# Columns 2 and 3 of Q, K and V in blocks 0 and 1 as seven block products

## The chip, the cores and the metric

The program runs on one core of one Trainium2 chip. The metric is the device time of one execution in microseconds (us). It is given as the median of three runs; a separate execution was taken with the hardware profiler.

## What is computed

One layer on x of 2048 tokens and 576 columns: a layer norm without weights, then sliding attention and a feed-forward part side by side, both added to x.

```
xn = (x - mean(x)) / sqrt(var(x) + 1e-5)
qkv = xn @ wqkv                       # 576 x 1728; 32 heads of 18 columns
# each token looks at itself and at the tokens 2, 4, ... 14 before it
o = softmax(q . k[idx] * 18 ** -0.5) @ v[idx]
h = relu(xn @ w1 + b1) ** 2           # 576 x 4608
out = x + o @ wo + h @ w2 + b2        # 4608 x 576
```

All values are float32. The products run in the type fp32r with each operand split into a high part (a copy in that type, made by ACT) and a low part (the rest, a subtraction on DVE). One product of A and W is then three matmuls: high by high, low by high and high by low.

## The kernel before

**Tiles.** The tokens are four blocks b of 512, and Q, K and V four groups g of 8 heads, 432 columns each (QW). The normalized block stands transposed in X[b], with 4 parts of 128 of the contraction (c), high and low, and in x4[b] with the 64 columns that are left over, high and low behind each other. The tokens j of 128 within a block are four column tiles. One (b, g, j) is a *row*: a PSUM tile of 128 tokens by 432 columns, made by 4 x 3 matmuls on X[b] and 2 on x4[b], 14 in all (row_products, qkv_row). ACT copies it out of PSUM (qkv_out, L358) and writes it to the array kvq in DRAM on its own DMA queue (L360). Attention reads it back from there.

**Order of work.** All engines run in the order in which the code is written. The function open_rows starts: it normalizes block 0 from rows and makes (0, 0), with TensorE transposes (L1434) and products (L1472). q0 follows, and makes in its list todo the rows of (0,1), (0,3), (0,2), (1,3), (1,2), (1,1) and (1,0), one at a time; behind each it takes steps of its list pieces: the statistics of block 1, the split of the weights of a group (split_wq), the normalization (normalize), the four sums for the feed-forward part (sums), and the left-over columns of the first feed-forward weights (left_w). The last two rows stand in the function filler and are made within the first feed-forward pair.

**Mean and scale of block 1.** statistics(1) makes mean and inverse deviation of each token, 4 rows of 128 tokens, on DVE and POOL. turn_mr transposes the 8 columns on TensorE (L204), ACT copies them out (L206), a DMA writes them to DRAM (L207), and load_mb (L213) reads them back in all 128 partitions, as the tile mb. normalize(1) subtracts and multiplies with mb.

**Block products.** The feed-forward part (ffn_pair, 18 pairs p for each half s of the tokens) computes 2 x 2 blocks with 7 products and not 8, named T1, B11, T2, T3, B21, B22 and T4 for the weights' block in each. sums(s) makes the sums of the tokens that they need (SS[1] to SS[3] and fourth_sum), left_x and left_w the same for the left-over columns, which are written to DRAM as a stack of seven (L612) and read again by load_stack (L619). For blocks 2 and 3, quad_step makes Q, K and V in the same way, for two groups at a time (k, which is 0 or 1) and a pair of column tiles (half) at a time: 14 steps of a product and a column tile, each product 6 matmuls, and 2 for the left-over columns in four of them (L1103, L1107). phase_b0 runs it; its lists say after which steps a piece of attention is taken.

**Attention.** One (b, g) is a generator of 19 pieces, nearly all on DVE; side(n) takes n of them, and in each feed-forward pair p of the first half PIECES[p] of them are taken ahead of the second product, with 4 more later in the pair. offer(b, g) queues one group, fetch loads its tiles when one of the three kv tiles is free.

**Loads around it.** On SP's queue stand, among others, the load of the left-over columns of w1 for the next four pairs (load_left_w, L626, into tile st), the load of the left-over x (load_left_x) and of the stacks, the loads of w1 and w2 (L500, L536), and the writes of the split w1 (L521).

## Time and profile before

| | us |
|---|---|
| median of three runs | 1102.49 |
| lowest, highest run | 1099.86, 1103.36 |
| span of the profiled execution | 1098.5 |
| TensorE busy in it | 1092.3 |
| DVE, ACT, POOL busy in it | 879.9, 563.2, 149.3 |

The span is one execution from the first instruction to the last. PE is TensorE's matmuls, PEld its weight loads, DVE the vector engine, ACT the scalar engine, POOL GpSimd, SP the engine that issues most DMAs; SPq, ACTq and POOLq are their DMA queues. A row of the timeline has the start, the duration (of several instructions together where it ends in x and a number), the engine, the line of the kernel and the tiles, out<-in. In brackets stands the idle time ahead of it and what ended it. A row of the groups has all instructions of one line and shape: busy time, mean duration in ns, and the idle time before them with what ended it. A row of a tile has the least, mean and greatest duration in ns. A row of the DMAs has the queue, the number of issues, the size of each and the median time from issue to landing. The granted clock of TensorE was full in this execution from the first slice to the last. The regions that the change touches are these:

```profile
0.00:20.90 20.90, 18.61 (x90) 14.12 (x91) 13.97 (x39) 12.15 (x27) 11.03 (x28) 1.00 0.86 312
20.90:92.40 71.50, 71.50 (x368) 68.59 (x367) 57.16 (x80) 30.94 (x53) 3.35 (x6) 1.00 0.77 257
92.40:109.20 16.80, 16.80 (x79) 14.62 (x78) 9.72 (x15) 9.41 (x15) 0.00 (x0) 1.00 0.66 232
109.20:141.50 32.30, 32.13 (x142) 26.18 (x141) 31.36 (x43) 22.16 (x29) 12.83 (x24) 1.00 1.02 341
```

The columns are the window and its length, the busy time of PE, PEld, DVE, ACT and POOL, the granted clock, the share of the DMA engines and GB/s. The first window is the start (open_rows), the second the rows of q0 but for the last two, the third the first feed-forward pair with those two rows, the last the two pairs behind it. TensorE waits 0.17 us in the fourth window and nothing in the second and third.

### The profile page before, as it was taken

To read this page: it belongs to the slowest core of one execution; us is meant where nothing else is said; L and a number is where in the kernel's file an instruction comes from. 1 tells how busy PE (TensorE), PEld (TensorE's weight loads), DVE (VectorE), ACT (ScalarE), POOL (GpSimd) and SP (SyncE) were. 2 spreads that over 40 slices of the span, in tenths; PEclk is the share of its full clock that TensorE was granted. 3 is DMA by queue.
4 is the path that set the end of the run, shared out by engine and by line. 5 is a ranking of instruction groups with operands and counts; after the bars stand their busy time and mean duration, and the time that the engine had idled before them with its cause. 6 is when DMAs were issued, how large, how long until landed. Compare 5 with 4: busy or idle time off the path is not lost.

```text
span 1098.5 us, 13947 instructions
## 1 busy us (share of the span) xinstructions
PE 1092.3 (99%) x4936; PEld 922.9 (84%) x4936; DVE 879.9 (80%) x1183; ACT 563.2 (51%) x794; POOL 149.3 (14%) x267
## 2 busy tenths in 40 slices
PE   9999999999999999999999999999999999999998
PEld 7999888888888888888899988888888888888887
DVE  7687988899898979999879387776767676889955
ACT  5435666656666654555344345454554545543432
POOL 4000401031030101003010300201101010101010
PEclk9999999999999999999999999999999999999999
DMA  8966998879989887868565988868686877685582
GB/s 282 340 221 214 342 391 314 338 268 257 393 317 294 317 332 261 306 225 315 197 211 168 320 318 284 305 224 315 222 294 221 294 241 288 224 284 194 185 290 83
DMA packets 109558, 298.97 MB, mean 272 GB/s; under 512 B 12648, under 2 KB 42736, under 8 KB 98608
## 3 DMA queue, kind: packets, MB, share of 16 engines
q1 hardware_dynamic: 69984, 192.84, 50.1%
q0 software_dynamic: 13200, 62.52, 16.2%
q10 hardware_dynamic: 26304, 42.71, 11.7%
q8 instruction: 39, 0.64, 0.2%
q14 instruction: 31, 0.25, 0.1%
HBM read 213.53 MB, written 84.50 MB: 271 GB/s over the span
## 4 chain that ended last, share of the span: by engine, by line
PE 99%; DVE 0%; ACT 0%; issue 0%; POOL 0%; ACTq 0%; POOLq 0%
PE p L573 47%; PE p L677 35%; PE p L366 7%; PE p L1103 6%; PE p L1107 1%; PE p L1472 1%; PE p L683 1%; PE p L1389 0%; PE p L1434 0%; DVE w1s L118 0%; ACT X L122 0%; PE p L1371 0%; ACT h L723 0%; DVE w2s L118 0%; DVE r L118 0%
## 5 line engine op out<-in xcount | busy, mean ns | idle before, releaser
L573 PE MATMUL p<-h,w2s 128*128 128x512 f32 x2066 | 491.6, 389 | 0.2 <-ACT h L723 0.2
L573 PEld LDWEIGHTS p<-h,w2s 128*128 128x128 f32 x2066 | 387.5, 188 | 81.7 <-ACT h L723 0.6
L677 PE MATMUL p<-X,w1s 128*128 128x512 f32 x864 | 219.2, 389 | 0.0
L677 PEld LDWEIGHTS p<-X,w1s 128*128 128x128 f32 x864 | 162.2, 188 | 33.5
L546 ACT ACTIVATE w2s<-w2r 128x640 fp32r<-128x640 f32 x164 | 120.3, 735 | 128.1 <-PE p L573 98.3
L118 DVE TENSOR_TENSOR w2s<-w2r,w2s 128x576 fp32r<-128x576 f32 x164 | 123.5, 753 | 72.3 <-ACT w2s L546 70.7
L677 PE MATMUL p<-S,w1s 128*128 128x512 f32 x648 | 164.5, 389 | 0.0
L677 PEld LDWEIGHTS p<-S,w1s 128*128 128x128 f32 x648 | 121.6, 188 | 25.1
L444 POOL DMA_DIRECT2D o<-q x128 | 69.5, 609 | 418.2 <-DVE q L118 416.7
L719 ACT ACTIVATE r<-r,b1t 128x512 f32<-128x512 f32 x72 | 52.2, 725 | 116.8 <-DVE r L118 115.7
L415 DVE TENSOR_REDUCE lg<-pr 128x64 f32<-128x1152 f32 x64 | 86.5, 1351 | 1.2
L118 DVE TENSOR_TENSOR pr<-lg,kv 128x1152 f32<-128x1152 f32 x64 | 86.6, 1354 | 1.0
L118 DVE TENSOR_TENSOR pr<-q,kv 128x1152 f32<-128x1152 f32 x64 | 86.6, 1354 | 0.9
L118 DVE TENSOR_TENSOR pr<-pr 128x576 f32<-128x576 f32 (+1 forms) x128 | 77.6, 606 | 3.5
L118 DVE TENSOR_TENSOR r<-p,r 128x512 f32<-128x512 f32 (+1 forms) x77 | 53.1, 689 | 32.8 <-ACT r L785 15.3
L727 ACT ACTIVATE r<-r 128x1024 f32<-128x1024 f32 x72 | 76.1, 1056 | 1.2
L118 DVE TENSOR_TENSOR h<-r,h 128x1024 fp32r<-128x1024 f32 (+3 forms) x46 | 51.8, 1135 | 23.4 <-ACT r L727 14.9
L761 ACT ACTIVATE r<-p 128x512 f32<-128x512 f32 x36 | 21.5, 598 | 82.1 <-PE p L677 82.1
L118 DVE TENSOR_TENSOR w1s<-w1r,w1s 128x1024 fp32r<-128x1024 f32 (+2 forms) x42 | 46.2, 1103 | 9.5 <-ACT w1s L515 8.8
L719 ACT ACTIVATE r<-p,b1t 128x512 f32<-128x512 f32 x72 | 48.2, 671 | 0.3 <-PE p L683 0.2
L118 DVE TENSOR_TENSOR h<-h 128x1024 fp32r<-128x1024 f32 x36 | 43.9, 1220 | 2.9 <-ACT h L1000 2.8
L573 PE MATMUL p<-w1s,w2s 128*128 128x512 f32 x195 | 44.7, 389 | 0.0
(207 smaller groups left out, 1166.7 us busy)
## 6 DMA issues: line engine op xcount, KB each, us to landing
w2r<-in_w SPq DMA_DIRECT2D x144, 320.0 KB, 3.9
kv<-kvq POOLq DMA_DIRECT2D x30, 1296.0 KB, 8.6
w<-w1s SPq DMA_DIRECT2D x21, 1024.0 KB, 8.5
w1s<-w ACTq DMA_DIRECT2D x19, 1024.0 KB, 5.9
h<-r SPq DMA_DIRECT2D x36, 512.0 KB, 6.2
h<-h SPq DMA_DIRECT2D x36, 512.0 KB, 4.1
w<-w1s SPq DMA_DIRECT2D x15, 768.0 KB, 10.3
w1s<-w ACTq DMA_DIRECT2D x15, 768.0 KB, 5.1
```

The lines of the kernel that those rows point to most:

```text
L118: return nc.vector.tensor_tensor(out=out, in0=a, in1=b, op=op)
L366: nc.tensor.matmul(p[:, :QW], l, r, start=k == 0, stop=k == len(mm) - 1)
L415: nc.vector.tensor_reduce(out=lg[:, j * HG:(j + 1) * HG].rearrange("p a w -> p w a"), in_=pr.rearrange("p w (a d) -> p w a d", d=DH), axis ...
L444: nc.gpsimd.dma_start(rows[:, i], q[i * L:(i + 1) * L, :, a:z])
L546: nc.scalar.activation(w2s[stream[i]][:, :DE], raw2[i], AF.Copy)
L573: nc.tensor.matmul(yp[b][c], v, a, start=c not in yb[b], stop=c in last and c not in [o[0] for o in ops[i + 1:]], skip_group_check=True)
L677: nc.tensor.matmul(to, l, r, start=start and i == 0, stop=i == len(mm) - 1, skip_group_check=True)
L683: nc.tensor.matmul(to, weight(LEFT, k, f), v, start=False, stop=k == 1, skip_group_check=True)
L719: nc.scalar.activation(to, a, AF.Relu, bias=b1t[:, f:f + 1])
L727: nc.scalar.activation(r, r, AF.Square)
L761: nc.scalar.activation(u[:, 0], bb, AF.Copy)
L1103: nc.tensor.matmul(to, l[:, js], r, start=start and n == 0, stop=n == len(mm) - 1, skip_group_check=True)
```

## The change

Rows (0,1), (1,1) and (1,0) stay plain and come first, and groups 2 and 3 of blocks 0 and 1 are then made by quad_step, with the new argument b0 = 0, in two halves of 14 steps. The last two steps of the second half stand in filler. The products' weights (B11, T1, T2, T3, B21, T4, B22 and the left-over columns) are made from the loaded weights of groups 2 and 3 within the third plain group (during_third) and the first half of the products (hook); sums(0) moves ahead, between the matmuls of (1,1), whose order is now by contraction part. Of each column tile's results, the row that needs a sum of two PSUM or staged values is written on POOL's queue for these blocks.

Mean and scale of block 1 take another way: spread_mr transposes, for each of the 4 columns of mr, that column repeated 128 times, so that the values stand in a PSUM bank in all partitions, and DVE reads them there. The statistics of block 1 start within open_rows.

The stack of left-over x is made in part 1 of pair 0 and part 0 of pair 1 (before: parts 0, 1 and 2 of pair 0), and read in part 2 of pair 1 (before: part 1); load_left_w goes from part 0 to part 1 of its pair. The order of attention's groups, PIECES and the lists of phase_b0 are set anew. In the diff, lines of only "..." mark what is left out.

```diff
-PIECES = (0, 1, 2, 2, 2, 2, 1, 3, 2, 2, 1, 1, 1, 0, 2, 2, 3, 3)
+PIECES = (0, 0, 1, 2, 2, 3, 1, 3, 2, 2, 1, 2, 1, 0, 2, 2, 4, 4)
...
-    def turn_mr(b, i):
+    def spread_mr(b, k, i):
         y = bank(i)
-        nc.tensor.transpose(y[:2 * NJ, :P], mrs[b].rearrange("p k j -> p (k j)"), ident)
-        t = sb.tile([2 * NJ, P], F32, name="mrt")
-        nc.scalar.activation(t, y[:2 * NJ, :P], AF.Copy)
-        nc.sync.dma_start(mrscr[b], t)
+        for j in range(NJ):
+            nc.tensor.transpose(y[:, j * P:(j + 1) * P], mrs[b][:, k, j:j + 1].to_broadcast([P, P]), ident)
+        mb.setdefault(b, {})[k] = y[:, None]
...
-                tt(v, v, mb[b][:, k:k + 1].to_broadcast([P, 2, TB]), op)
+                tt(v, v, mb[b][k].to_broadcast([P, 2, TB]), op)
...
-        e = fourth_sum[s] = four()
+        e = fourth_sum[s] = four() if s else sb.tile([P, 2, TB], F32, name="mb")
...
-            r = raws[g, k] = sb.tile([P, 2, QW], F32, name="r4", bufs=4)[:, :n]
+            r = raws[g, k] = (sb.tile([P, DE], F32, name="w2r", bufs=3)[:, None, :QW] if n == 1 and g > 1 else
+                              sb.tile([P, 2, QW], F32, name="r4", bufs=4)[:, :n])
...
-            if p == 0:
-                if i == 0:
-                    rv["x of"] = left_x(0)
-                next(rv["x of"])
-            if p == 1 and i == 1:
+            if (p, i) == (0, 1):
+                rv["x of"] = left_x(0)
+            if (p, i) in ((0, 1), (1, 0)):
+                for _ in range(1 + p):
+                    next(rv["x of"])
+            if (p, i) == (1, 2):
                 load_stack(0, sb.tile([P, 5, TB], F32R, name="kv", bufs=3), 0)
                 load_stack(0, sb.tile([P, 1, TB], F32R, name="xf"), 5)
...
-            if i == 0 and p % G == 1 and G * r < NP:
+            if i == 1 and p % G == 1 and G * r < NP:
                 load_left_w(r, sb.tile([P, 2 * NS, P], F32, name="st"))
...
-    QKV_BANKS = [(2, 3, 4), (5, 6, 7)]
+    QKV_BANKS = {2: [(2, 3, 4), (5, 6, 7)], 0: [(5, 6, 7), (2, 3, 4)]}
...
+    def quad_step(k, s, j, i, b0=2):
+        b1, gs = b0 + 1, (2 * k, 2 * k + 1)
+        if (b0, i) not in quad_banks:
+            quad_banks[b0, i] = [bank(n)[:, :QW] for n in (*QKV_BANKS[b0][i], i)]
+        a, b, c, u = quad_banks[b0, i]
...
-            (nc.scalar if y is None else nc.gpsimd if "last" in stage else nc.sync).dma_start(to, st.rearrange("p (i c) -> p i c", c=CG))
+            (nc.scalar if y is None else nc.gpsimd if "last" in stage or not b0 else nc.sync).dma_start(to, st.rearrange("p (i c) -> p i c", c=CG))
...
-                if n in ((2, 3, 4, 6, 8, 10, 12), (3, 6, 8, 10, 12, 13), (1, *range(3, 14)), ())[2 * k + half]:
+                if n in ((1, 2, 3, 4, 6, 8, 10, 11, 12), (0, 2, 6, 8, 10, 12, 13), (2, 3, 5, 6, 7, 8, 9, 10, 11, 12, 13), (0,))[2 * k + half]:
                     side(1)
                 hook(k, half, s, i)
...
         normalize_rows(3, nm)
+        next(of_rows)
         out(1)
...
+    def plain_rows(b, g, banks, at=lambda j, k: None):
+        for j, i in enumerate(banks):
+            p = bank(i)
+            mm = row_products(b, g, j)
+            for k, (l, r) in enumerate(mm):
+                at(j, k)
+                nc.tensor.matmul(p[:, :QW], l, r, start=k == 0, stop=k == len(mm) - 1)
+            qkv_out(b, g, j, p, 0)
+            at(j, len(mm))
+
     def q0():
-        todo = [(b, g, j) for b, g in ((0, 1), (0, 3), (0, 2), (1, 3), (1, 2), (1, 1), (1, 0)) for j in range(NJ)]
-        pieces = [statistics(1), split_wq(3, "S")]
...
-            if r == 2:
-                turn_mr(1, 7)
-                run_all(pieces)
-                load_wq(2)
-                load_mb(1)
-            if r == 1:
-                load_left_w(0, sb.tile([P, 2 * NS, P], F32, name="w1r", bufs=2))
-            if r == 4:
-                pieces += [split_wq(2, "h", lambda: load_wq(0)), normalize(1), left_w(0)]
...
+        some(of_rows, 3)
+        norm = normalize(1)
+
+        def during_first(j, k):
+            if j == 2 and k in (4, 8):
+                spread_mr(1, k // 8, (5, 7)[k // 8])
+            if (j, k) == (2, 14):
+                some(norm, 4)
+
+        plain_rows(0, 1, range(4), during_first)
+        some(norm, 4)
+        load_wq(2, (1, 2))
...
+        load_w1(0)
+        free[0] -= 1
+        kept_back[0] = 0
+        stage[1] = kv_tile(NJ * QW).rearrange("p (j c) -> p j c", c=QW)
...
+        def open_slot(name):
+            if name == T4:
+                ws[name] = [mt.tile([P, DE + D], F32R, name="w2s", bufs=3)[:, :2 * QW].rearrange("p (c n) -> p c n", c=2)
+                            for _ in range(2)]
+            else:
+                t = mt.tile([P, 2, 2, TB], F32R, name="w1s" if name in (B11, T1, T2) else "h", bufs=3)
...
+        def hi(name, v):
+            open_slot(name)
+            nc.scalar.activation(ws[name][0], v, AF.Copy)
+
+        def lo(name, v):
+            tt(ws[name][1], v, ws[name][0].bitcast(F32), ALU.subtract)
...
+        for cs in ((0, 1), (2, 3)):
+            for j in range(NJ):
+                for c in cs:
+                    for y in range(2):
+                        mm(j, c, 0, y, start=c == y == 0)
+        parts = sums(0)
+        some(parts, 1)
+        for j in range(NJ):
+            for c in range(NC - 1):
+                mm(j, c, 1, 0)
+            for y in range(2):
+                mm(j, NC - 1, 0, y, stop=y == 1)
+            qkv_out(1, 1, j, p[j], 1)
+            if j in (0, 2):
+                some(parts, 2)
+        of_w = left_w(0)
+        hi(B11, b11)
+        some(parts, 2)
+        some(of_w, 1)
+        lo(B11, b11)
+        lane[0] = nc.gpsimd
+
+        def during_third(j, k):
+            if k < 3 * NC - 1:
+                return
+            if j == 0:
+                tt(b11, b12, b11, ALU.subtract)
+                hi(T1, b11)
+                tt(b12, b22, b12, ALU.subtract)
+                some(of_w, 1)
+                ws[LEFT, 0] = mt.tile([P, DE + D], F32R, name="w2s", bufs=3)[:, :2 * QW].rearrange("p (k c) -> p k c", c=QW)
+                side_hi(0)
+            if j == 1:
+                lo(T1, b11)
+                tt(b11, b22, b11, ALU.subtract)
+                hi(T2, b11)
+                some(parts, 1)
+            if j == 2:
+                lo(T2, b11)
+                some(parts, 1)
+                some(of_w, 1)
+                release()
                 offer(0, 0)
...
-            if r == 17:
-                load_left_x(0, kv_tile(2 * NS * P).rearrange("p (s t) -> p s t", t=P))
-            if r == 19:
...
+            if j == 3:
+                some(parts, 1)
+
+        plain_rows(1, 0, (3, 4, 0, 1), during_third)
+        load_w1(1)
...
+        def hook(half, s, i):
+            at = half, s, i
+            if at == (0, 1, 0):
+                hi(B21, b21)
+                lo(B21, b21)
+            if at == (0, 1, 1):
+                hi(T3, b12)
+                side_lo(0)
+                lo(T3, b12)
+                ws[LEFT, 1] = four(F32R)[:, :, :QW]
+                side_hi(1)
+            if at == (0, 2, 1):
+                side_lo(1)
+                tt(b11, b21, b11, ALU.subtract)
+                hi(T4, b11)
+            if at == (0, 3, 0):
+                some(parts, 1)
+                lo(T4, b11)
+            if at == (0, 3, 1):
+                some(parts, 1)
+                hi(B22, b22)
+            if at == (0, 5, 0):
+                lo(B22, b22)
+                nc.scalar.activation(X[1][:, 0, :2], fourth_sum[0], AF.Copy)
+            if at == (0, 4, 0):
+                tt(X[1][:, 1, :2], fourth_sum[0], X[1][:, 0, :2].bitcast(F32), ALU.subtract)
+            if at == (0, 6, 1):
                 for n in range(3):
                     load_w2(n)
+            if at == (1, 1, 1):
+                offer(0, 1)
+            if at == (0, 7, 0):
                 combine_w1(0)
-                load_w1(1)
-            if r in (23, 24):
-                w1_hi(0, r - 23)
-                w1_lo(0, r - 23)
-            elif r not in (3, 22):
-                run(pieces, 3 if r < 1 or 14 <= r < 20 else 1 if r > 20 else 2)
+            if at == (1, 4, 0):
+                w1_hi(0, 0)
+                w1_lo(0, 0)
+            if at == (1, 4, 1):
+                w1_hi(0, 1)
+                w1_lo(0, 1)
...
+        def quads(half, which):
+            for n in which:
+                s, i = steps[n]
+                quad_step(1, s, 2 * half + i, i, 0)
+                if n in ((13,), (2, 3, 6, 8, 10, 12))[half]:
+                    side(1)
+                hook(half, s, i)
+
+        quads(0, range(len(steps)))
+        quads(1, range(len(steps) - 2))
+        load_left_x(0, sb.tile([P, 2 * NS, P], F32, name="st"))

         def filler(i):
             if i < 2:
-                row(len(todo) - 2 + i)
+                quads(1, [len(steps) - 2 + i])
             if i == 1:
-                last_sum(0)
+                for b, g in ((0, 2), (0, 3), (1, 1), (1, 0), (1, 2), (1, 3)):
+                    offer(b, g)

...
+    of_rows = statistics(1)
     open_rows()
     for g in range(G):
         for k in "kv":
             nc.gpsimd.dma_start(scr[k][g][:PAD], zero)
-    load_wq(3)
-    free[0] = 2
+    load_wq(2, (0,))
+    load_wq(3, (0,))
+    load_left_w(0, kv_tile(2 * NS * P).rearrange("p (s t) -> p s t", t=P))
+    free[0] = 1
```

The places in the order of each engine, which is the order of the code, with line numbers of the kernel before and after and with the names of tiles:

TensorE, ahead of the last rows of (0,1); before (X_230 and x_231 are X[0] and x4[0], p_530 is the bank of turn_mr, S_507 a weight tile of group 3):

```order
L366 MATMUL p_513<-w1s,X_230 128x432 x12
L366 MATMUL p_513<-w1s,x_231 128x432 x2
L204 MATMUL p_530<-mb,mr 8x128
L366 MATMUL p_546<-w1s,X_230 128x432 x12
L366 MATMUL p_546<-w1s,x_231 128x432 x2
L366 MATMUL p_564<-S_507,X_230 128x432 x6
```

The same place after (p_509 and p_518 are the banks of spread_mr, X_531 is X[1]):

```order
L1540 MATMUL p_504<-w1s,X_229 128x432 x4
L205 MATMUL p_509<-mb,mr 128x128 x4
L1540 MATMUL p_504<-w1s,X_229 128x432 x4
L205 MATMUL p_518<-mb,mr 128x128 x4
L1540 MATMUL p_504<-w1s,X_229 128x432 x4
L1540 MATMUL p_504<-w1s,x_230 128x432 x2
L1540 MATMUL p_539<-w1s,X_229 128x432 x12
L1540 MATMUL p_539<-w1s,x_230 128x432 x2
L1595 MATMUL p_575<-w1s,X_531 128x432 x4
```

One transpose behind the third row has become eight within the third row, and block 1's rows stand directly behind the fourth.

ACT in the first half of the products, after (p_759 and p_773 are the sums of the two column tiles' first product, p_760 and p_774 the copies that the next products add to, L1105 copies the sum with T2's product; r_ tiles are loaded weights, h, w1s and w2s their high parts):

```order
L1100 ACTIVATE p_760<-p_759 128x432
L1578 ACTIVATE h<-r_563 128x2x432
L1100 ACTIVATE p_774<-p_773 128x432
L1578 ACTIVATE h<-r_442 128x2x432
L1584 ACTIVATE r_788<-w2r 128x432
L1578 ACTIVATE w2s<-r_440 128x864
L1105 ACTIVATE p_762<-p_760 128x432
L250 ACTIVATE x4d<-w2r 128x512
L1105 ACTIVATE p_776<-p_774 128x432
L1578 ACTIVATE h<-r_567 128x2x432
L1091 ACTIVATE st<-p_759 128x432
L1095 DMA kvq_98<-st 128x3x144
```

Before, ACT had at this stage only the rows' copies, their writes, and the high parts of the sums; now the copies out of PSUM and the high parts of the weights for the products that follow stand in one order.

SP in the first feed-forward pairs, before (L521 writes the split w1, L536 and L500 load w2 and w1, L737 writes the squares):

```order
L521 DMA w_114<-w1s 128x2048
L626 DMA st<-in_w1l 128x512
L737 DMA h_158<-r_1154 128x1024
L536 DMA w2r<-in_w 128x640
L521 DMA w_115<-w1s 128x2048
L536 DMA w2r<-in_w 128x640
L500 DMA w1r<-in_w 128x1024
L521 DMA w_116<-w1s 128x2048
L619 DMA kv<-stk_151 64x2560 x2
```

and after:

```order
L497 DMA w_114<-w1s 128x2048
L512 DMA w2r<-in_w 128x640
L476 DMA w1r<-in_w 128x1024
L497 DMA w_115<-w1s 128x2048
L602 DMA st<-in_w1l 128x512
L595 DMA kv<-stk_150 64x2560 x2
L595 DMA xf<-stk_150 64x512 x2
L620 DMA mb<-lw_152 128x1x896
L714 DMA h_158<-r_1270 128x1024
```

The load of st has moved from behind one write of the split w1 to behind two, and the reads of the stack now follow it directly.

More of the change, by code (lines that the diff above doesn't have):

```diff
@@ L99, in block_kernel @@
     oscr = {(b, k): dram.tile([P, NJ * G, z - a], F32, name=f"o{b}{k}") for b in range(NB) for k, (a, z) in enumerate(OPART)}
-    mrscr = {b: dram.tile([2 * NJ, P], F32, name=f"mr{b}") for b in range(1, NB)}
+    mrscr = {b: dram.tile([2 * NJ, P], F32, name=f"mr{b}") for b in range(2, NB)}
     def slots(n, k):
@@ L326, in wq_lo @@
         tt(wq[g, k][:, :, 1], raws[g, k], wq[g, k][:, :, 0].bitcast(F32), ALU.subtract)
-    def split_wq(g, name, then=lambda: None):
-        open_wq(g, name)
-        for k in range(4):
-            if k < 3:
-                wq_hi(g, k)
-            if k:
-                wq_lo(g, k - 1)
-                if k == 3:
-                    then()
-                    split_up.add(g)
-                yield
     qp, stage = {}, {}
@@ L360, in qkv_out @@
         nc.scalar.dma_start(to, st.rearrange("p (i c) -> p i c", c=CG))
-    def qkv_row(b, g, j, i, places):
-        p = bank(i)
-        mm = row_products(b, g, j)
-        for k, (l, r) in enumerate(mm):
-            nc.tensor.matmul(p[:, :QW], l, r, start=k == 0, stop=k == len(mm) - 1)
-        qkv_out(b, g, j, p, places)
     def shifted(t, j, *dims):
@@ L1256, in hook @@
                 fetch()
[L1258 removed]
+        steps = quad_steps
         def quads(k, half, some):
```

81 lines of the change are left out of this document (27 added, 54 removed).

## The prediction

> **What bounds the kernel now.** I read the page's busy shares first, then its chain, then the chain in order of time.
>
> ```profile
> span 1098.5 us, 13947 instructions
> PE 1092.3 (99%) x4936; PEld 922.9 (84%) x4936; DVE 879.9 (80%) x1183; ACT 563.2 (51%) x794; POOL 149.3 (14%) x267
> PE 99%; DVE 0%; ACT 0%; issue 0%; POOL 0%; ACTq 0%; POOLq 0%
> ...
> 29.24 63.05 PE p L366 x322
> ```
>
> The chain that ends last is TensorE for 99%: every other engine is ready in time nearly everywhere. So the time is the number of matmuls times their interval, plus the few places where PE waits. A matmul of 432 columns takes 63.05/322 = 0.1958 us; a copy of the new scheme already runs later in this program (blocks 2 and 3), and there a half of it, 100 matmuls, takes as long:
>
> ```profile
> 542.46 8.22 PE p L1103 x42
> 562.04 8.23 PE p L1103 x42
> ```
>
> 562.04 - 542.46 = 19.58 us, 0.1958 each, without a wait. That is the pace to expect of the new products, if their operands come in time.
>
> **Matmuls removed.** Groups 2 and 3 of blocks 0 and 1 were 4 combinations of 4 rows of 14 matmuls, 224. As block products they are 4 column tiles of 7 x 6 + 8 = 50, so 200. 24 x 0.1958 = **-4.70 us**, all on the path.
>
> **Transposes added.** Eight 128x128 transposes come, one with 8 columns goes.
>
> ```profile
> 16.60 0.76 PE L1434 MATMUL p<-mb,kv 128*128 128x128 f32 x5
> 17.12 0.64 PE L1472 MATMUL p<-h,X 128*128 128x432 f32 x2
> ...
> 28.97 0.27 PE L204 MATMUL p<-mb,mr 128*8 128x128 f32 x1
> 29.00 2.58 PE L366 MATMUL p<-w1s,X 128*128 128x432 f32 x12
> ...
> 31.81 2.51 PE L366 MATMUL p<-S,X 128*128 128x432 f32 x12
> ```
>
> Five of the same shape and type hold PE from 16.60 to 17.12, 0.104 each, so eight cost 0.83. The old one took 29.00 - 28.97 = 0.03, and the row behind it 31.81 - 29.00 = 2.81 for 14 x 0.1958 = 2.74: 0.10 goes. Net **+0.74**. The new weights are one column repeated 128 times, which no row shows; the bounds are nothing and the 0.27 that one stands as busy (8 x 0.27 = 2.2), and I take the value of the like shape. The Trainium skill, "FP8 and Floating Point Precision", section "TensorE Precision Notes", says that true FP32 takes four passes through the array; with a pass of 128 columns estimated from the 432-column row, 0.058, eight would cost 1.9 and the sum below would be 1.1 worse. The trace disagrees for transposes: 0.104 is no four passes.
>
> **Block 1's mean and scale.** Each row of statistics costs DVE 23.59 - 22.37 = 1.22:
>
> ```profile
> 18.11 0.69 DVE L118 TENSOR_TENSOR X<-p,X 128x512 fp32r<-128x512 f32 x1 [2.14 <-ACT X L122]
> 22.37 0.81 DVE L145 BATCH_NORM_STATS2 st<-kv 128x6 f32<-128x288 f32 x2
> 23.59 0.81 DVE L145 BATCH_NORM_STATS2 st<-kv 128x6 f32<-128x288 f32 x2
> ...
> 6.53 0.49 SPq L160 DMA_DIRECT2D kv<-in_x  x1
> kv<-in_x SPq DMA_DIRECT2D x1, 1152.0 KB, 8.7
> 20.74 2.52 PE L366 MATMUL p<-w1s,X 128*128 128x432 f32 x12
> 39.44 4.88 DVE L118 TENSOR_TENSOR w1r<-w1r,mb 128x1024 f32<-128x1024 f32 x4 [0.16 <-DMA mb<-mr]
> ```
>
> One row moves into DVE's idle 2.14 us ahead of 18.11. Its data land at 6.53 + 8.7 = 15.2, and DVE is free from 18.11 - 2.14 = 15.97: hidden, with 0.8 us to spare; if the data were late, the split for PE would be as late. The other three end at 22.37 + 3 x 1.22 = 26.0. PE starts group 1 at 20.74, reaches the first four transposes after 32 matmuls at 27.0 and the others at 28.2: both find their numbers. The two small DMAs and the 512 KB load go, so DVE normalizes at 27.7 and not at 39.44. It takes 1.22 for each of four pieces: the first high half is there at 27.7 + 2.44 + 1.06 (ACT) = 31.3, and PE, after 56 matmuls and eight transposes, asks at 32.5. The later halves have over 1 us too. Cost nothing; if the normalization slips by more than 1.2 us, PE waits for all of the excess.
>
> **The first half of the new products.** They begin at 20.74 + 168 x 0.1958 + 0.74 = 54.4. Here operands are made while they are used, and ACT and DVE pass a chain to and fro:
>
> ```profile
> L323 ACT ACTIVATE h<-r 128x864 fp32r<-128x864 f32 x4 | 3.6, 922 | 1.0 <-DMA r<-in_wqkv 0.4 <-ACT st L358 0.4
> L118 DVE TENSOR_TENSOR h<-r,h 128x864 fp32r<-128x864 f32 x4 | 4.1, 1056 | 6.8 <-ACT h L323 6.8
> L118 DVE TENSOR_TENSOR r<-mb,r 128x432 fp32r<-128x432 f32 x4 | 2.4, 602 | 0.0
> ...
> L1127 ACT ACTIVATE p<-p 128x432 f32<-128x432 f32 x8 | 4.0, 511 | 9.7 <-PE p L1103 9.1 <-DVE q L118 0.7
> L251 ACT ACTIVATE x4d<-w2r 128x512 fp32r<-128x512 f32 x1 | 0.6, 632 | 3.9 <-DVE w2r L118 3.9
> L271 ACT ACTIVATE S<-r 128x1024 fp32r<-128x1024 f32 x2 | 2.1, 1062 | 2.9 <-DVE r L118 2.4 <-PE p L366 0.5
> L358 ACT ACTIVATE st<-p 128x432 f32<-128x432 f32 x24 | 12.6, 526 | 16.1 <-PE p L366 14.3 <-ACT st L358 1.4 <-PE p L1472 0.3
> L360 ACTq DMA_DIRECT2D kvq<-st x24: 366/366/404, 15.1 to 102.7; - x24
> ```
>
> The first product's sum is out at about 55.75: six matmuls, and some 0.2 until ACT starts. Behind it stand ACT's copy 0.51, B21's high half 0.92, three low parts on DVE (1.06, 0.60, 1.06), the left-over weights' high and low (0.53, as the other 432-column copies, and 0.60), B21 - B11 (1.06), T4's high half (0.92), and only then the copy of T2's sum (0.51): 7.8 us, so 63.55. PE asks for that bank after six products, eight matmuls and two more: 54.4 + 46 x 0.1958 = 63.4. With the 0.22 that PE takes to restart (113.80 to 114.02 in the rows below) it waits 0.4. Behind the copy on ACT stand 0.63, 0.51, 0.92, 0.53, 0.37, 1.06 and 0.53, 4.6 us with gaps, until the bank of T3's sum is read at 68.2; PE wants it at 68.1, and waits 0.3. Together **+0.7**; the bounds are nothing (19.58 us per half above) and about 1.5, if each operation starts 0.05 later.
>
> **The first feed-forward pairs.** PE enters them about 3.2 us earlier. In pair 1 ACT is already last:
>
> ```profile
> 112.28 1.90 PE L573 MATMUL p<-h,w2s 128*128 128x512 f32 x7 [0.17 <-ACT h L723]
> 113.22 0.58 ACT L746 ACTIVATE p<-p 128x512 f32<-128x512 f32 x1
> L424 ACT ACTIVATE lg<-lg 128x256 f32<-128x256 f32 x16 | 6.5, 409 | 19.3 <-DVE lg L118 14.4 <-DMA kvq<-st 4.9
> ...
> 114.02 1.55 PE L677 MATMUL p<-S,w1s 128*128 128x512 f32 x6
> ```
>
> PE was ready at 112.28 + 7 x 0.2267 = 113.87 and waited until 114.02. The attention of group 0 is later now, and its exponential stands ahead of that copy: **+0.4**; nothing if DVE and ACT gain elsewhere, 1.4 if DVE reaches its reduction a microsecond late.
>
> The left-over stack is written one part later, so SP stands at the load of st until the writes land:
>
> ```profile
> 110.09 4.37 POOL L612 DMA_DIRECT2D stk<-kv  x8 [31.12 <-ACT kv L590]
> 124.93 1.44 SPq L619 DMA_DIRECT2D kv<-stk  x2
> st<-in_w1l SPq DMA_DIRECT2D x4, 256.0 KB, 4.6
> x4d<-stk SPq DMA_DIRECT2D x2, 128.0 KB, 17.8
> 141.90 1.14 SPq L619 DMA_DIRECT2D x4d<-stk  x2
> 160.75 0.39 PE L677 MATMUL p<-x4d,mb 128*128 128x512 f32 x1
> ```
>
> From first write to read took 14.8 us. Now ACT frees the first at about 112.4, SP goes on at 127.2, st lands at 131.8; DVE, waiting in order with w2's stores and loads queued behind on SP, needs 3.5 us more to w2's low half, which PE wants at about 135.6. Cost 0, or up to 2 with 1.7 us of delay more.
>
> Eight row writes move to POOL, 0.75 us each there, on an engine 14% busy. DVE gains some 10 us of work in all and attention starts 8 us later; against that stand 1098.5 - 879.9 = 219 us in which DVE is idle, so I cost it at nothing: it is spread over several pairs. If it is not, its exponentials are late in the pairs that follow, and PE waits there as in pair 1.
>
> **Sum.** -4.70 + 0.74 + 0.7 + 0.4 = -2.9, so a span of 1095.6. The profiled span lies 4.0 below the median, 1102.49; I carry the difference over: **1099.6**.
>
> **Rivals.** *Count alone*: the chains keep up, as the later copy does. -4.70 + 0.74 = -3.96: 1098.5. For it: 19.58 us per half; against: that copy's operands were ready beforehand.
> *The transfer stays*: x4d lands at 141.9 + 17.8 = 159.7, its second part later, and PE uses it at 160.75. If the backlog of DMA and not PE sets the landing, PE comes 3 us early and waits: about 1102.5.
> *Slower*: the load of the left-over x waits for the last row writes, now POOL's, and DVE stands at its sums ahead of the first pair's result.
>
> ```profile
> kvq<-st ACTq DMA_DIRECT2D x32, 216.0 KB, 4.0
> kvq<-st POOLq DMA_DIRECT2D x2, 216.0 KB, 7.8
> kvq<-w1r ACTq DMA_DIRECT2D x2, 216.0 KB, 17.2
> st<-xl SPq DMA_DIRECT2D x2, 128.0 KB, 5.0
> ```
>
> The row is issued at about 89.8; with 7.8, SP's issue and 5.0 the data are there near 104, and DVE comes at 105.4. From a landing of 9 us on, each microsecond costs PE one; with 17.2 it is 8: 1107.7. The Trainium skill, "DMA: Bandwidth & Descriptors", section "Issuing engine by pattern", says that the queues of SP and ACT are generally faster than GpSimd's. The rows agree, 4.0 against 7.8.
>
> **Chances.** A run can tell about 0.3%, 3.3 us, from no change. Forecast 0.50 (0.18 of it beyond 3.3, since 2.9 lies so near), count alone 0.27 (0.20 beyond), transfer 0.12 (0.02 slower), slower 0.11. So faster 0.38, same 0.49, slower 0.13. Half the spread of the runs shown is (1103.36 - 1099.86) / 2 = 1.75. The range runs from count alone less this, 1096.8, to the transfer and its wait with this on top, 1104.3; it takes in the ends of the unknown costs in the forecast (waits of nothing, or 1.5 and 1.4 in the two places) and leaves out most of the slower case.
>
> **What would show it.** 24 matmuls of 432 columns fewer; eight transposes in under 1 us; a half of the products in 20.3 us the first time and 19.58 the second; waits of PE for ACT's copies in the first half and in pair 1, none for w2's low half in pair 2 nor for x4d in pair 3. A half that takes 19.58 at once, or any wait of PE over 1 us, makes this wrong.

## The result and the profile after

The changed kernel takes 1126.73 us, the median of 5 runs (1125.35 to 1128.06), against 1099.86 for the kernel before in the same session: a ratio of 1.0233, 95% interval 1.0218 to 1.0248. It is slower, where a gain of 2.9 us was forecast, and lies 22 us above the range. One execution in all, of the kernel below that has the row writes on SP's queue, took 2235.14 us, twice as long as the others of that kernel, and its ratio leaves it out. The page of the changed kernel's profiled execution, beside that of before:

```profile
span 1126.2 us, 13956 instructions
PE 1099.2 (98%) x4919; PEld 926.4 (82%) x4919; DVE 888.3 (79%) x1195; ACT 566.9 (50%) x801; POOL 153.2 (14%) x278
PE 79%; DVE 8%; DMA 6%; issue 5%; ACT 1%; POOL 0%; SPq 0%; DVEq 0%; POOLq 0%; ACTq 0%
```

The chain that ends last was TensorE for 99% and is now TensorE for 79%, with DVE and DMA in it. And PE is busy for longer, 1099.2 us against 1092.3, though it has fewer matmuls to do: by the count it should be 1092.3 - 4.70 + 0.74 = 1088.3. So two things were added, waits and slower matmuls. The list of what PE waits for (line waited at, releaser, total, times, longest):

```profile
PE p L653 <- DVE r L118: 17.8, 3, 9.4
PE p L1081 <- DVE h L957: 3.2, 1, 3.2
```

These are 21.0 us, where the kernel before had 0.2 in this part of the program (both have 2.1 at the start). With 1099.2 - 1088.3 = 10.9 us of slower matmuls this makes 31.7: the spans differ by 27.7, and the removed work of 4.0 is hidden in it. The 10.9 takes that removed work as forecast; the kernels further down, which no longer have these waits, have PE busy for 1089.7 to 1090.1 us, and beside them the slower matmuls come to 9.1 to 9.5.

The new products themselves are not the cause. Their two halves, and the new transposes, in the timeline of PE:

```profile
25.99 0.94 PE L1540 MATMUL p<-w1s,X 128*128 128x432 f32 x4
26.77 0.60 PE L205 MATMUL p<-mb,mr 128*128 128x128 f32 x4
27.12 1.02 PE L1540 MATMUL p<-w1s,X 128*128 128x432 f32 x4
...
29.58 2.53 PE L1540 MATMUL p<-w1s,X 128*128 128x432 f32 x12
...
54.26 2.52 PE L1081 MATMUL p<-w1s,X 128*128 128x432 f32 x12
73.90 2.50 PE L1081 MATMUL p<-w1s,X 128*128 128x432 f32 x12
```

The first half takes 73.90 - 54.26 = 19.64 us, as much as the copy for blocks 2 and 3. The row with the eight transposes in it takes 29.58 - 25.99 = 3.59, which is 0.85 more than its 14 matmuls of 0.1958; 2 x 0.35 of this stands at the transposes, the rest at the matmuls behind them.

Where the waits stand, the timeline shows. First the largest. In the kernel before, SP issues the load of the left-over w1 columns for the next four pairs (L626) in part 0 of pair 9, and DVE uses it 16 us later:

```profile
255.90 0.33 SPq L626 DMA_DIRECT2D st<-in_w1l  x1
...
271.85 1.26 DVE L118 TENSOR_TENSOR st<-st 128x128 f32<-128x128 f32 x4
```

The same place after the change, where the load (now L602) stands in part 1:

```profile
262.38 0.33 SPq L497 DMA_DIRECT2D w<-w1s  x1
...
264.52 1.23 SPq L476 DMA_DIRECT2D w1r<-in_w  x1
...
265.80 0.98 SPq L497 DMA_DIRECT2D w<-w1s  x1
...
267.22 0.56 SPq L602 DMA_DIRECT2D st<-in_w1l  x1
...
285.52 1.27 DVE L118 TENSOR_TENSOR st<-st 128x128 f32<-128x128 f32 x4 [12.04 <-DMA st<-in_w1l]
...
291.18 2.93 PE L653 MATMUL p<-X,w1s 128*128 128x512 f32 x6 [9.38 <-DVE r L118]
```

The load is issued 11.3 us later and now comes behind the load of w1 for the pair three on and the writes of the split w1. DVE is ready for it at 273.5, stands 12 us, and all that is queued behind on DVE is late, the sums of PE's results among it: PE waits 9.4 us in pair 10. The same happens in pair 14 (PE waits 5.6). The chain of the changed kernel has the two transfers on it (start, time, from issue to landing):

```profile
267.22 18.18 DMA st<-in_w1l
...
346.67 15.63 DMA st<-in_w1l
```

The second place is pair 0:

```profile
93.70 1.81 SPq L576 DMA_DIRECT2D st<-xl  x2
...
107.50 1.27 DVE L118 TENSOR_TENSOR st<-st 128x128 f32<-128x128 f32 x4 [3.19 <-DMA st<-xl]
...
109.42 2.93 PE L653 MATMUL p<-S,w1s 128*128 128x512 f32 x6 [2.83 <-DVE r L118]
112.15 3.19 PE L549 MATMUL p<-h,w2s 128*128 128x512 f32 x7
```

DVE has the left-over x 13.8 us after its first issue, where the row of before that the prediction used has 5.0 for such a load, and PE waits 2.8 us. The landing of the two loads, from issue:

```profile
st<-xl SPq DMA_DIRECT2D x2, 128.0 KB, 13.2
```

The third place is the end of block 1's sums, ahead of the products of blocks 2 and 3:

```profile
549.14 0.75 POOL L364 DMA_DIRECT2D kv<-kvq  x1
...
553.16 0.54 POOL L364 DMA_DIRECT2D kv<-kvq  x1
553.17 0.33 SPq L512 DMA_DIRECT2D w2r<-in_wo  x1
553.55 0.42 SPq L943 DMA_DIRECT2D h<-in_xt  x1
...
567.04 0.74 ACT L522 ACTIVATE w2s<-w2r 128x640 fp32r<-128x640 f32 x1 [5.19 <-DMA w2r<-in_wo]
...
569.41 2.53 PE L1081 MATMUL p<-r,X 128*128 128x432 f32 x6 [3.20 <-DVE h L957]
```

The loads of attention's next group (L364) stand here now, among the last output weights. In the kernel before such a load was issued here:

```profile
506.19 0.55 POOL L388 DMA_DIRECT2D kv<-kvq  x1
```

That is 36 us ahead of the products. Attention writes its sixth group at 545 us, and did so at 422 before; its loads fall into another place.

### The profile page after: what moved, and what is told of

Its sections match the earlier page's. It is cut to its first block, busy times and chain, and to the rows that moved or that the text cites. A ratio compares the mean times of both kernels' runs of the same rounds, so it can differ in the third digit from the quotient of the medians.

```text
span 1126.2 us, 13956 instructions
## 1 busy us (share of the span) xinstructions
PE 1099.2 (98%) x4919; PEld 926.4 (82%) x4919; DVE 888.3 (79%) x1195; ACT 566.9 (50%) x801; POOL 153.2 (14%) x278
## 4 chain that ended last, share of the span: by engine, by line
PE 79%; DVE 8%; DMA 6%; issue 5%; ACT 1%; POOL 0%; SPq 0%; DVEq 0%; POOLq 0%; ACTq 0%
PE p L549 39%; PE p L653 30%; PE p L1081 6%; DMA st<-in_w1l 3%; DVE pr L118 1%; PE p L1085 1%; DVE w1r L118 1%; PE p L1450 1%; DVE w2s L118 1%; DVE w1s L118 1%; DMA st<-xl 1%; PE p L659 1%; DMA xf<-in_xt 1%; DVE r L118 1%; PE p L1540 1%
## 5 line engine op out<-in xcount | busy, mean ns | idle before, releaser
L653 PE MATMUL p<-X,w1s 128*128 128x512 f32 x864 | 224.2, 396 | 14.9 <-DVE r L118 14.9
L653 PEld LDWEIGHTS p<-X,w1s 128*128 128x128 f32 x864 | 165.4, 192 | 50.3 <-DVE r L118 15.8
L118 DVE TENSOR_TENSOR w2s<-w2r,w2s 128x576 fp32r<-128x576 f32 (+1 forms) x165 | 124.0, 752 | 75.2 <-ACT w2s L522 75.1
L118 DVE TENSOR_TENSOR h<-r,h 128x1024 fp32r<-128x1024 f32 (+2 forms) x43 | 49.8, 1163 | 10.9 <-ACT r L704 8.6
L118 DVE TENSOR_TENSOR w1s<-w1r,w1s 128x1024 fp32r<-128x1024 f32 (+2 forms) x42 | 46.2, 1102 | 10.6 <-ACT w1s L491 10.2
```

The source lines that it names most:

```text
L118: return nc.vector.tensor_tensor(out=out, in0=a, in1=b, op=op)
L653: nc.tensor.matmul(to, l, r, start=start and i == 0, stop=i == len(mm) - 1, skip_group_check=True)
```

## The experiments

Each kernel was timed in alternation with the kernel before, which took 1100.2 to 1100.3 in these sessions.

**The load back in part 0.** The changed kernel with one condition:

```diff
-            if i == 1 and p % G == 1 and G * r < NP:
+            if i == (p == 1) and p % G == 1 and G * r < NP:
```

> The changed kernel with the load of the left-over weights (st from w1l) put back to part 0 of its pair for pairs 5, 9 and 13; pair 1 keeps part 1. Theory Q (the load is issued about 11 us later than before, behind the load of w1 and the writes of the split w1, lands 18.2 and 15.6 us later and holds DVE, and with it PE, in pairs 10 and 14): both waits of PE, 9.4 and 5.6 us, go, and with each some 2.7 us in which the matmuls behind a wait run at half pace; 1126.7 - 15.0 - 5.4 = about 1106. Theory R1 (DVE is late by attention's pieces, the load's landing only coincides): within 2 us of 1126.7.

It took 1104.49 us (ratio 1.0052, interval 1.0032 to 1.0073). 22.2 us of the loss go with this line; PE has no wait left in pairs 10 and 14. R1 falls, and of theory Q it is shown that the load's move makes the two waits; whether by its later issue or by what then stands ahead of it, this edit doesn't part.

**The same edit alone, in the kernel before.**

```diff
-            if i == 0 and p % G == 1 and G * r < NP:
+            if i == 1 and p % G == 1 and G * r < NP:
```

> The kernel before with one edit of the change alone: the load of the left-over weights in part 1 of its pair instead of part 0. Theory Q: the same two waits arise without any new product, 1099.9 + 15 + 5.4 = about 1120. Theory R1: nothing is lost, within 2 us of 1099.9.

It took 1129.98 us (ratio 1.0272, 1.0256 to 1.0287): without any new product the kernel before loses 29.7 us, more than forecast, since pair 2 waits there too (7.9 us). Its list of waits:

```profile
PE p L677 <- DVE r L118: 23.0, 3, 8.4
```

**The load in part 1, on ACT's queue.**

```diff
-        nc.sync.dma_start(v[:, :4], w1l[i])
+        (nc.scalar if i > 1 else nc.sync).dma_start(v[:, :4], w1l[i])
```

> The changed kernel, load of the left-over weights in part 1 as there, but issued on ACT's queue for pairs 5, 9 and 13 (and pair 1 as it is numbered among the later loads only from the second on). If the place behind 2 to 3 MB on SP's queue makes the landing 18 us, it lands within about 6 us here and both waits go: about 1106. If the DMA engines as a whole are behind at that time, whichever queue, the landing stays at 15 us or more and the time at 1122 to 1127.

It took 1106.92 us (1.0058, 1.0041 to 1.0076). PE's waits at this line fall from 17.8 to 3.6 us, of which 2.9 are pair 0's. The load stands in the same part, but on ACT's queue it is issued ahead of the load of w1 and the second write of the split w1, 4.2 us earlier than in the changed kernel in pair 9. It lands after 12.1 us, and DVE still waits for it; the median of its three landings on that queue stands in the last row:

```profile
263.03 0.35 ACTq L602 DMA_DIRECT2D st<-in_w1l  x1
...
275.23 1.27 DVE L118 TENSOR_TENSOR st<-st 128x128 f32<-128x128 f32 x4 [2.52 <-DMA st<-in_w1l]
...
st<-in_w1l ACTq DMA_DIRECT2D x3, 256.0 KB, 12.1
```

So both cases of the expectation missed: the time is that of the first, and the landing, 6.9 us in pair 5 and 12.1 and 12.5 in pairs 9 and 13, lies between its 6 and 15. PE hardly waits for it, since it was issued earlier and landed 3 to 6 us sooner. How much of this is the queue and how much the issue ahead of the other transfers is not parted here. The Trainium skill, "DMA: Bandwidth & Descriptors", section "Queues, rings and completion order", says that each DMA engine goes round between the queues that have work for it. The rows don't contradict this: between 225 and 280 us ACT's queue carries nothing but this load, and it still lands after 12.1 us, beside SP's transfers.

**The left-over x one part later.** Its first sums on DVE in part 2 of pair 0:

```diff
-            if (p, i) == (0, 1):
+            if (p, i) == (0, 2):
                 rv["x of"] = left_x(0)
-            if (p, i) in ((0, 1), (1, 0)):
+            if (p, i) in ((0, 2), (1, 0)):
```

> The changed kernel with the first piece of the left-over x (DVE's sums that need st from xl) in part 2 of pair 0 instead of part 1. If the load's landing (107.5 us) is all that holds DVE there, PE's wait of 2.8 us goes and 2.7 us of half pace behind it: about 1121. If DVE then stands at the same sums one part later, or its other work of that pair is late, less than 2 us are gained.

It took 1120.6 us (1.0188, 1.0173 to 1.0203): 6.1 us go, near the 5.5 expected, and in part by luck: the waits in pairs 10 and 14, which the edit was not meant for, are 12.5 us together and not 15.0. And its waits show a new one, which is of the kind that the prediction has for pair 1: attention's exponential stands ahead of ACT's copy, and DVE comes to it later.

```profile
PE p L653 <- ACT p L723: 2.0, 1, 2.0
```

**Both.** The edits of the two kernels above with the early load:

> The load of the left-over weights early again (as in e1_w_early) and the first piece of the left-over x in part 2 of pair 0 (as in e2_x_later). If the two losses are separate, the gains add: 1126.7 - 22.2 - 6.1 = about 1098.4. If they are one backlog, less is gained: above 1102.

1105.12 us (1.0045, 1.0033 to 1.0057): the second case. The gain of the second edit is not there once the first is made. In the profile PE waits 2.6 us for that copy in pair 1 and 2.9 ahead of the products of blocks 2 and 3; the loss had moved by a part, and the third place had grown.

**The left-over x on ACT's queue**, on top of the early load:

```diff
-            nc.sync.dma_start(v[:, places], dims(xlscr[2 * s + k], 0, [P, P], [L * TB, 2], [1, P]))
+            (nc.sync if s else nc.scalar).dma_start(v[:, places], dims(xlscr[2 * s + k], 0, [P, P], [L * TB, 2], [1, P]))
...
-        load_left_x(0, sb.tile([P, 2 * NS, P], F32, name="st"))
...
                 quads(1, [len(steps) - 2 + i])
+            if i == 0:
+                load_left_x(0, sb.tile([P, 2 * NS, P], F32, name="st"))
```

> As e1_w_early, with the left-over x loaded on ACT's queue, issued behind the first of the last two steps of the products, and used in part 1 of pair 0 as in the changed kernel. Theory: what made that load land 10 to 13 us after its issue is its place on SP's queue behind the load of w1 and two writes of the split w1; on ACT's queue it lands in about 5 us, PE's wait of 2.6 us in pair 0 goes with its half pace: 1104.5 - 5.5 = about 1099. Rival (the row writes on POOL's queue hold the tile too long): the load is issued at about 94 all the same and PE still waits; 1102 to 1105.

1104.52 us (1.0037, 1.0023 to 1.0051), with runs from 1100.92 to 1108.77. PE's wait for DVE in pair 0 is gone from the profile, but a wait of 1.6 us for ACT stands in its place, since ACT issues the two loads from 96.35 on for 2.0 us, ahead of its copies; and 2.5 us stand ahead of the products of blocks 2 and 3. There is no gain, and the theory is half right at most: on ACT's queue the loads land after 9.3 and 8.6 us, not after 5.

**Fewer pieces of attention** in pairs 16 and 17, on top of that:

```diff
-PIECES = (0, 0, 1, 2, 2, 3, 1, 3, 2, 2, 1, 2, 1, 0, 2, 2, 4, 4)
+PIECES = (0, 0, 1, 2, 2, 3, 1, 3, 2, 2, 1, 2, 1, 0, 2, 2, 2, 2)
```

> As e6_x_on_actq, with 2 pieces of attention taken in pairs 16 and 17 ahead of the second product instead of 4. This puts off the next group's loads (two of 1296 KB on POOL's queue, at 527 and 531 us in e1_w_early) behind the last loads of the output weights ahead of the products of blocks 2 and 3. If their traffic is what makes PE wait there (1.7 us in e1_w_early), that wait goes: 2 us below e6. If not, or if the pieces are then missing later, within 1 us of e6 or above it.

1103.36 us (1.0027, 1.0018 to 1.0036), too near to the last to tell. The loads moved from 527 and 531 to 534 and 540 us, which is still among the output weights; PE waits 2.1 us there. This did not test the theory.

**The row writes on SP's queue**, with the early load and nothing else:

```diff
-            (nc.scalar if y is None else nc.gpsimd if "last" in stage or not b0 else nc.sync).dma_start(to, ...)
+            (nc.scalar if y is None else nc.gpsimd if "last" in stage else nc.sync).dma_start(to, ...)
```

> As e1_w_early, with the eight row writes that the change puts on POOL's queue on SP's queue. If their time on POOL's queue is what makes the load of the left-over x late (rival in the prediction), st is free about 1 us earlier and PE's wait of 2.6 us shrinks by that: about 1102 to 1103.5. If the place on SP's queue is the cause, no change within 1 us of 1104.5, or worse, since SP waits for DVE ahead of its loads.

1104.41 us (1.0039, 1.0026 to 1.0052): the same time as with the early load alone. The parts are not the same, though: PE's waits for DVE fell from 2.6 to 0.7 us in all, and the wait ahead of the products of blocks 2 and 3 is 3.1 where it was 1.7. In pair 0 by itself PE's wait fell from 2.62 to 0.42 us: the loads of the left-over x are issued 0.4 us earlier or 0.9 later, and land after 11.9 and 10.6 us where 13.3 stood. That what was won early was lost later is argued and not shown, since the profiled execution with the early load took 1102.73 us, 1.8 less than the median of that kernel. The stretch ahead of that wait, first in this kernel and then in the kernel before (window, busy times of PE, PEld, DVE, ACT and POOL, granted clock, DMA share, GB/s):

```profile
530.00:540.00 10.00, 10.00 (x45) 8.28 (x45) 8.89 (x9) 2.78 (x4) 0.63 (x2) 1.00 0.96 373
```

```profile
530.00:540.00 10.00, 10.00 (x45) 8.28 (x45) 7.94 (x12) 4.71 (x7) 0.00 (x0) 1.00 0.58 210
```

The DMA engines are full there now, 0.96 against 0.58. That gave theory C.

**Attention's loads held back** until the products begin, on top of the last:

```diff
             if n == 34:
                 slot_lo(B21, raw[0, 1][:, 0])
+            if n == 24:
+                kept_back[0] = 3
...
         stage[1] = kv_tile(NJ * QW).rearrange("p (j c) -> p j c", c=QW)
+        lane[0] = nc.sync
+        fetch()
+        lane[0] = nc.gpsimd
```

> As e8_rows_on_spq, with the loads of attention's next group (K, Q and V, at 525 to 530 us there on POOL's queue) put off until the products of blocks 2 and 3 begin, on SP's queue behind the loads of the output weights. Theory C (these loads, 2.9 MB, take the DMA engines while the last output weights come in, and that is what makes PE wait 3.1 us ahead of the products, with some 2.5 us of half pace behind it): the wait goes, 1104.4 - 5 = about 1099. If attention then stands without its data and holds DVE, PE waits within the products instead: 1102 or more. If other traffic is the cause: 1104.

1099.44 us (0.9997, 0.9988 to 1.0006): 5 us go, and PE has no wait ahead of the products in the profile. This bears theory C out.

**More pieces of attention**, the other way to the same end, also on top of the row writes:

```diff
-PIECES = (0, 0, 1, 2, 2, 3, 1, 3, 2, 2, 1, 2, 1, 0, 2, 2, 4, 4)
+PIECES = (0, 0, 2, 2, 2, 3, 2, 3, 2, 2, 2, 2, 2, 1, 2, 2, 4, 4)
```

> As e8_rows_on_spq, with five more pieces of attention in the first half (one more in pairs 2, 6, 10, 12 and 13), so that the sixth group ends earlier and the next loads come about 20 us ahead of 525, as in the kernel before (505). Theory C: PE's wait ahead of the products of blocks 2 and 3 goes, about 1099. If DVE can't take the pieces in these pairs, PE waits there: 1105 or more.

1102.16 us (1.0016, 1.0005 to 1.0026), between the two. In the profiled execution the wait ahead of the products is gone here too; 1.2 us stand in pair 0. But this execution took 1099.63 us, the least of runs that spread to 1104.83, so where the median's 2.5 us more stand is not shown.

**The left-over x ahead of w1's transfers.** On top of the held loads, the load of w1 for pair 2 and the write of the split w1 are issued behind the load of the left-over x, not ahead of it:

```diff
-    def w1_lo(n, k):
-        tt(w1s[n, k][:, 1], raw1[n][:, 4 * k:4 * k + slots(n, k)], w1s[n, k][:, 0].bitcast(F32), ALU.subtract)
+    def w1_lo(n, k, moves=True):
+        if moves is not None:
+            tt(w1s[n, k][:, 1], raw1[n][:, 4 * k:4 * k + slots(n, k)], w1s[n, k][:, 0].bitcast(F32), ALU.subtract)
+        if moves is False:
+            return
...
                 w1_hi(0, 1)
-                w1_lo(0, 1)
+                w1_lo(0, 1, False)
...
         load_left_x(0, sb.tile([P, 2 * NS, P], F32, name="st"))
+        w1_lo(0, 1, None)
```

> As e9_loads_held, with the left-over x's load issued on SP ahead of the load of w1 for pair 2 and the write of the split w1, and not behind them. Theory: their 1.6 MB are what makes it land 10 us after its issue; it lands in about 5 us, PE waits no more in pair 0 in any run, and the count of the matmuls shows: a span near 1098.5 - 4.0 = 1094.5 and a median of 1096 to 1097.5, with a smaller spread than e9's 4.4 us. Rival (the load of w1 for pair 2, now 4 us later, is missed): PE waits in pair 1 or 2, 1099 or more.

1097.92 us (0.9979, 0.997 to 0.9988), with runs from 1097.3 to 1099.64: faster than both kernels, by 0.2% beside the one before, and a spread of 2.3 us and not 4.4. It takes 1.5 us less than the kernel with the held loads; the two intervals just touch. Its timeline, with the landing of the two loads behind their row:

```profile
93.17 1.57 SPq L579 DMA_DIRECT2D st<-xl  x2
st<-xl SPq DMA_DIRECT2D x2, 128.0 KB, 3.2
...
104.84 1.27 DVE L118 TENSOR_TENSOR st<-st 128x128 f32<-128x128 f32 x4
...
108.61 1.89 PE L552 MATMUL p<-h,w2s 128*128 128x512 f32 x7
110.49 1.67 PE L656 MATMUL p<-S,w1s 128*128 128x512 f32 x6
```

and its list of waits, but for the start:

```profile
PE p L656 <- DVE r L118: 0.4, 1, 0.4
```

The loads are issued 0.5 us earlier than in the changed kernel and land after 3.2 us instead of 13.2, and DVE no longer waits for them. The wait that is left stands in pair 2, behind a wait of DVE for the left-over w1 of pair 1, which is the place that the prediction priced:

```profile
131.15 1.27 DVE L118 TENSOR_TENSOR st<-st 128x128 f32<-128x128 f32 x4 [3.83 <-DMA st<-in_w1l]
...
137.06 1.65 PE L656 MATMUL p<-X,w1s 128*128 128x512 f32 x6 [0.40 <-DVE r L118]
```

The median is a little above what was expected, 1096 to 1097.5.

**The same with the row writes on POOL's queue**, as the change has them:

```diff
-            (nc.scalar if y is None else nc.gpsimd if "last" in stage else nc.sync).dma_start(to, ...)
+            (nc.scalar if y is None else nc.gpsimd if "last" in stage or not b0 else nc.sync).dma_start(to, ...)
```

> As e12_x_ahead, with the eight row writes on POOL's queue again, as the change has them. If the place on SP's queue was the whole cause in pair 0, the same time as e12 within 1 us. If the writes on POOL's queue hold the tile too long by themselves (rival in the prediction), the load is issued 1 to 1.5 us later and PE waits 0 to 1.5 us: up to 3 us above e12.

1098.81 us (0.9982, 0.9973 to 0.9991). The intervals of the two overlap, and PE has no wait in pair 0: once the loads stand ahead of w1's transfers (they land after 3.6 and 5.0 us), POOL's queue costs nothing there. Its profile does have 1.5 us in pair 2 where the last had 0.4, again behind DVE's wait for the left-over w1 of pair 1.

## Why the prediction was wrong

*Matmuls removed*: right. The changed kernel's own sums can't show it, since its slower matmuls were reckoned with it. The kernel with the left-over x ahead of w1's transfers shows it, up to the same matmuls of pair 0. The plain rows behind open_rows begin at 20.74 before and at 20.98 there; in pair 0, before and then there:

```profile
103.32 0.62 PE L683 MATMUL p<-x,w1s 128*128 128x512 f32 x2
```

```profile
99.79 0.62 PE L662 MATMUL p<-x,w1s 128*128 128x512 f32 x2
```

103.32 - 20.74 = 82.58 and 99.79 - 20.98 = 78.81: 3.77 us saved, where 4.70 - 0.74 = 3.96 were counted. At the end a span of 1098.5 - 1096.3 = 2.2 us is left of it.

*Transposes*: right. Eight cost 0.85 us with the matmuls behind them, where 0.83 was reckoned; a column repeated 128 times is no slower than the like shape.

*Block 1's mean and scale*: right, no wait of PE stands there.

*The first half of the products*: mis-sized. It was to cost 0.7 more than the later copy, and cost 73.90 - 54.26 - 19.58 = 0.06. The chain between ACT and DVE came a little sooner than reckoned: the copy of T2's sum ends at 62.64 + 0.52 = 63.16, 8.90 behind the products' begin, where 9.15 was reckoned and PE asks after 46 x 0.1958 = 9.0.

*Pair 1*: its wait could be seen only when pair 0 no longer hid it. In the kernel with the left-over x ahead PE starts T3 at 110.49 where 108.61 + 7 x 0.2267 = 110.20, so 0.3 us. Before it waited 0.15 there, so some 0.15 came where 0.4 more was forecast; where the left-over x's sums were put a part later, the wait for that copy was 2.0 us.

*The load of st, the left-over w1*: this is the step that failed. The prediction priced the move of this load in pair 1 alone, "Cost 0, or up to 2 with 1.7 us of delay more". The edit is a condition on the pair modulo 4: it moves the loads of pairs 5, 9 and 13 too, no row of those pairs was read, and they stand in the sum at nothing. In pair 9 the load was issued 6 us behind SP's last transfer before and landed after 4.2; issued 11.3 us later, behind w1's transfers, it takes 18.2, and in pair 13 15.6. The edit alone costs the kernel before 29.7 us, and its undoing in these three pairs gives the changed kernel 22.2 back. In pair 1 the price was about right: with the other waits gone the load lands at 131.0 where 131.8 was reckoned, and PE waits 0.4 to 1.5 us in pair 2.

*The slower rival* was real and came on top: DVE stood at the left-over x's sums in pair 0 and PE waited 2.8 us. Its place was right, its mechanism for the most part not. The row write that it feared landed 4.6 us after its issue at 89.11, sooner than its 7.8, and the load was issued at once; it is the load itself that took 13.2 us and not 5.0. Either edit takes nearly the whole wait away: the row writes on SP's queue (2.62 to 0.42 us), or the load ahead of w1's transfers, with the row writes on POOL's queue as they were (to nothing). And a wait of 2.8 us costs half pace behind it as well, which the price left out.

*Attention eight microseconds later, hidden over several pairs*: wrong in size and form. Its first group is written at 148.9 us where before at 125.8, and in the kernel with the held loads, where PE hardly waits, at 143.7: 18 us late. DVE did take up the delay, and no exponential made PE wait in the later pairs. But attention's sixth group ended at 545 us and not at 422, and the loads that follow it fell among the last output weights. Holding them back gave 5 us.

*The transfer stays* (x4d in pair 3): did not occur, no wait of PE stands there.

What stays open: whether the wait of pair 0 and that ahead of blocks 2 and 3 trade against each other (the second was 1.7 and then 3.1 us, in one execution each), and how much of the late landings is the order on SP's queue and how much the other transfers of that time. And of the 3.77 us saved up to pair 0, 2.2 are left at the end. About 0.6 goes in pair 2 with the wait of 0.4. Another 0.9 goes without any wait of PE: from 137.06 to the products of blocks 2 and 3 at 540.40 the kernel with the left-over x ahead takes 403.34 us, and the kernel before 402.40 for the same matmuls, from 139.90 to 542.30. No run shows why.

## What to carry to other kernels

The landing time of a transfer belongs to what is issued ahead of it, and not to its size alone: here the same 256 KB landed after 4.2 and after 18.2 us. Before a load is moved, read what will stand ahead of it, on its own queue first, and compare the time from issue to use with that. An edit within a condition on a loop's index is to be looked up in every turn in which it holds, since the margins differ from turn to turn: here the load of pair 5 made no wait, and those of pairs 9 and 13 cost 22 us. And where work is put off as a whole, follow its loads to where they will fall; the engine that has room for the work says nothing of the transfers.

## What the runs showed of the hardware

A wait of PE costs more than its length. Behind the wait of 2.83 us in pair 0 six matmuls took 2.93 us and the next seven 3.19 us, about twice the usual 1.52 and 1.75. In the chain of the changed kernel, behind the wait of 9.38 us and at an undisturbed place:

```profile
291.18 5.87 PE p L653 x14
...
306.64 3.18 PE p L653 x14
```

The granted clock is 0.50 for the 10 us around the end of this wait:

```profile
286.20:296.30 10.10, 5.12 (x12) 4.07 (x13) 10.03 (x13) 3.10 (x5) 1.09 (x2) 0.50 0.63 202
```

The four waits cost 9.1 to 10.9 us in this way, 2.3 to 2.7 each, about half of what they cost by themselves on top. Not every wait does. In the kernel with fewer pieces a wait of 2.05 us was followed by matmuls at about half pace (six of this shape take 1.35 us elsewhere), and in that with the left-over x one part later a wait of 1.99 us was not (1.52 elsewhere); nor was one of 1.69 us in the kernel with the early load:

```profile
545.13 2.53 PE L1081 MATMUL p<-r,X 128*128 128x432 f32 x6 [2.05 <-DVE h L957]
```

```profile
111.91 1.66 PE L653 MATMUL p<-S,w1s 128*128 128x512 f32 x6 [1.99 <-ACT p L723]
```

```profile
546.04 1.43 PE L1081 MATMUL p<-r,X 128*128 128x432 f32 x6 [1.69 <-DVE h L957]
```

The Trainium skill, "TensorE: Matmul & The Clock Gate", section "What's actually happening", says that the clock falls to half after an idle window of about 3.4 us. The rows agree in the half and in its lasting a few microseconds; they differ in the threshold, since 2.05 us of idle time were enough here.
